# A fused sort-attention and feed-forward kernel: the first two chunks' calls in a new order

## The chip, the cores and the metric

The kernel runs on one core of one Trainium2 chip. The metric is the device time of one execution in microseconds (us), as the median of several runs. Before the change it is 232.17 us (three runs, 232.09 to 232.53). One further execution was recorded by the hardware profiler; every duration below comes from that one.

The core has five engines that run side by side, each with its own list of instructions that it works off in order: PE (matrix products, into the accumulator memory PSUM), DVE (elementwise work and reductions), ACT (activation functions and copies), POOL (memory fills, gathers of columns, and the start of most loads) and SP (which only starts DMAs). They wait for each other by semaphores. DMAs run on 16 DMA engines; those that POOL starts stand in one queue, those that SP starts in another.

## The reference

```python
P = sort_net                                  # 4 batches x 8 heads x 8 x 8
for _ in range(5):                            # balancing
    P = exp(P - max(P, -1)); P /= sum(P, -1); P /= sum(P, -2)
k_sorted = einsum('bhij,bhjcd->bhicd', P, k)  # 8 blocks of 96 keys, mixed by P
v_sorted = einsum('bhij,bhjcd->bhicd', P, v)
scores = q_block @ k_sorted_block.T / 8       # within each block of 96
attn = softmax(scores)
x = (attn @ v_sorted), heads side by side     # 3072 x 512
h = x @ w_in                                  # 512 x 2048
out = (h * cos(h)) @ w_out                    # 2048 x 512
```

## The kernel before, in words

The 3072 output rows are made in eight chunks of 384 rows (`n` = 0 to 7; two chunks to a batch). A chunk has four units `u` of 96 rows, which are one block of the attention over all eight heads.

For each unit: scores on PE (`s_ps`), their maximum and the subtraction on DVE (`s_max`, `s_sub`), the exponential on ACT (`expo`), a transposition on PE (`p_ps`) that ACT or DVE copies out of PSUM (`p_ev`), the product with the values on PE (`av_products`), the division on DVE (`av_norm`), and a second transposition (`x_ps`, `x_ev`), which leaves the unit's 96 columns in `xT`. For each chunk then the first feed-forward product `h` on PE, its cosine on ACT, the product of both on DVE (`gg`), and the second product `o`, whose result ACT or DVE copies and SP stores. In chunk 0 the first product is cut into halves of 192 columns: `up_four(h, g, part)`, with `h` = 0 for units 0 and 1 and `h` = 1 for units 2 and 3; `cos_four` and `gate_four` follow, and `down_four` is a quarter of the second product.

Keys and values are sorted by PE too. `kp` makes the first batch's sorted keys (48 products), which `k_place` copies from PSUM, `v0` the first batch's values (copied out by `v0e`), `ks` the second batch's keys (`kse`), and `v_sort_b` the second batch's values. Values of the upper half of the columns are first gathered into rows by POOL (`v_permute`).

The order of the work up to the second feed-forward stage is a list of calls, written out by hand: each call puts its instructions at the end of the lists of the engines it uses. PSUM tiles come from two pools, `big` (three buffers, `*B`) and `acc` (two buffers, `*C`); a call that takes a buffer waits until its last user is done. Behind that list, loops over chunks (`moe_up`, `moe_down`) with fixed slots give the order; they are not touched.

What the list of calls also sets is the order in which POOL starts loads: keys `kbuf` and values `vbuf` (both are parts of `kv`), the queries of chunk 1, 2 and 3 (`load_q`, the last in eight pieces), `w_in` and `w_out` in quarters, and the keys and values of batches 2 and 3 (`pair`, and thirds of `kv`). The built program gives eight semaphores in turn to the DMAs that POOL starts, so a DMA start carries a wait for the landing of the DMA that stood eight places before it. POOL also clears what must be zero: `z_turned(z)` clears the unused halves of `q_turned[z]`, the turned queries of every second chunk, which the full-height scores read (lines 142 to 145), `p_pads` the pads of the probability buffers (743), `z_vperm` the half of `vperm` (739), `zeros_between` the gaps between the queries of chunk 3 (137). `q_turned[0]` holds chunk 0's queries and, from `q_transpose(2, ...)` on, chunk 2's; its first full-height reader is `qk_half(2, 0, 0)`, behind `up(1, 2)` in the untouched part.

`keep_warm(times, ...)` issues products of a tile of zeros with itself; a `fill` argument of a call does so in that call's PSUM tile before its own products.

Of the kernel before, what the change touches and what calls it, by code (L numbers as in the profile page):

```python
# [10 lines left out]
FP32 = mybir.dt.float32  # L11
# [7 lines left out]
def kernel(  # L19
# [15 lines left out]
    nc = tc.nc  # L35
# [12 lines left out]
    IC = 4  # L48
# [698 lines left out]
    def kp(t, pool, tag, fill=0):  # L747
        o = ps["k", t] = pool.tile([128, 16, 2 * NB], FP32, name="ks", tag=tag)
        keep_warm(fill, o[:, :8].rearrange("p t n -> p (t n)"))
        for z in range(16):  # L750
            k_products(o, z, t * 16 + z, slice(0, 128),
                       bds[0][:, H:].rearrange("p x i -> p (x i)"))

    def k_place(t, eng, half=None):
        lo, hi = (0, nb) if half is None else (half * IC, half * IC + IC)
        o = ps["k", t]
        copy_on(
            eng, kT[0].rearrange("p z (h i) t -> p z h i t", i=nb)[
                :, ::2, :, lo:hi, t * 16:t * 16 + 16],
# [147 lines left out]
    v_permute(slice(0, 64), 48, False, 8, 56)  # L907
    v_permute(slice(0, 64), 56, False, 8, 64)
    k_place(2, A, 1)
    k_place(2, V, 0)  # L910
    kp(1, *B)
    k_place(0, A, 0)
    blocks.append(block([pick[:, :, z * PB:(z + 1) * PB] for z in (1, 0)]))
    k_place(1, V, 0)
    k_place(1, A, 1)
    values_matrix()
    k_place(0, A, 1)
    s_ps(0, 0, fill=3)
    v0(4, *C)
    s_max(0, 0)  # L920
    v0(0, *B)
    v0e(4, A)
    s_sub(0, 0)
    s_ps(0, 3)
    v0e(0, A)
    v0(5, *C)
    s_max(0, 3)
    load_w_out(0)
    v0e(5, A)
    s_ps(0, 1)  # L930
    load_w_out(1)
    load_w_out(2)
    load_w_out(3)
    v0(6, *C)
    ones(0)
    expo(0, 0, True)
    s_ps(0, 2)
    s_sub(0, 3)
    v0(1, *C)
    v0e(6, A)  # L940
    s_max(0, 1)
    expo(0, 3, True)
    v0(3, *B, fill=2)
    s_sub(0, 1)
    v0e(1, A)
    p_ps(0, 0, *C, fill=2)
    v0e(3, A)
    s_max(0, 2)
    v0(7, *C)
    expo(0, 1, True)  # L950
    kxp(2)
    v0(2, *B, fill=1)
    p_ev(0, 0, V)
    v0e(7, A)
    s_sub(0, 2)
# [299 lines left out]
```

## Time and profile before

| | before |
|---|---|
| median of three runs | 232.17 us (232.09 to 232.53) |
| the profiled execution's own time | 231.61 us |
| its span, first to last instruction | 229.8 us |
| PE busy | 220.8 us, 96% of the span |
| DVE, ACT, POOL busy | 170.8, 154.4, 96.1 us |
| start of the untouched part, `up(1, 0)` | 56.3 us |

The page of the profile gives busy time by engine, the chain of work that ended last, and the costliest groups of instructions. In a timeline, each row has the start, the duration, the engine, the source line and the operation with its tiles (out<-in), and in brackets the idle time of that engine before it with what ended it. A row with "x8" merges eight neighbours of a kind. "DMA to landing" is the time from the start on the issuing engine to the last byte.

### The profile page before, as it was taken

The numbers are of one execution on the slowest core, as the hardware profiler recorded it, in microseconds if no ns is written. First come the engines' busy times: TensorE is split into PE (matmuls) and PEld (weight loads), VectorE is DVE, ScalarE is ACT, GpSimd is POOL, SyncE is SP. The second block draws the span as 40 slices with busy tenths as digits, with TensorE's granted clock in tenths as the row PEclk, the third lists the DMA queues.
The fourth block names the chain that finished last, engine by engine and source line by source line (L and its number), as shares of the span: only waits on it lengthen the run. The fifth ranks groups of instructions, "written<-read, shape, count | busy, mean of one in ns | idle before, by whom it ended". The sixth has DMA issues, their size and how long they took to land.

```text
span 229.8 us, 5513 instructions
## 1 busy us (share of the span) xinstructions
PE 220.8 (96%) x2245; PEld 138.7 (60%) x2268; DVE 170.8 (74%) x291; ACT 154.4 (67%) x207; POOL 96.1 (42%) x121
## 2 busy tenths in 40 slices
PE   8788999999999999999999999999999999999994
PEld 3378898567765566655665456655655565556554
DVE  6769968978698778868489977987699769646700
ACT  5659877777889858797688466736674667716521
POOL 7999999399950197943609000800000000000000
PEclk9999999999999999999999999999999999999999
DMA  6999999994999799667979939964924440351012
GB/s 83 225 187 207 202 206 236 195 227 148 124 124 191 171 139 148 118 135 146 162 118 163 135 74 148 210 98 81 206 92 80 90 160 0 69 147 46 0 46 94
DMA packets 67833, 31.21 MB, mean 136 GB/s; under 512 B 56416, under 2 KB 63200, under 8 KB 67552
## 3 DMA queue, kind: packets, MB, share of 16 engines
q0 software_dynamic: 24048, 13.64, 43.3%
q1 hardware_dynamic: 43472, 17.02, 35.1%
q8 instruction: 18, 0.29, 0.5%
q10 hardware_dynamic: 288, 0.20, 0.3%
q14 instruction: 7, 0.06, 0.1%
HBM read 27.27 MB, written 6.29 MB: 146 GB/s over the span
## 4 chain that ended last, share of the span: by engine, by line
PE 90%; DVE 3%; POOL 2%; issue 1%; ACT 1%; POOLq 0%; ACTq 0%
PE h L672 32%; PE o L697 30%; PE h L860 5%; PE o L881 4%; PE av L628 4%; PE sc L441 3%; PE ks L408 2%; PE o L1219 2%; PE pps L838 1%; PE sc L507 1%; PE xps L659 1%; PE vs L785 1%; PE vs L452 1%; PE qps L268 1%; PE xps L847 1%
## 5 line engine op out<-in xcount | busy, mean ns | idle before, releaser
L672 PE MATMUL h<-xT,w_in_t 128*128 128x384 bf16 x448 | 78.4, 326 | 0.1
L697 PE MATMUL o<-w_out_t,gg 128*128 128x512 bf16 x303 | 73.7, 379 | 1.0 <-issue 0.3
L676 ACT ACTIVATE c<-h,half_pi 128x768 f32<-128x768 f32 x56 | 50.5, 902 | 26.0 <-PE h L672 25.0
L680 DVE TENSOR_TENSOR gg<-c,h 128x768 bf16<-128x768 f32 x56 | 52.7, 949 | 19.5 <-ACT c L676 19.5
L672 PEld LDWEIGHTS <-w_in_t 128*128 128x128 bf16 x448 | 42.2, 98 | 26.3 <-DVE xT L259 0.6
L697 PEld LDWEIGHTS <-gg 128*128 128x128 bf16 x320 | 29.0, 99 | 28.3
L573 ACT ACTIVATE p_buf<-s 96x768 bf16<-96x768 f32 x32 | 26.6, 843 | 5.2 <-DVE s L494 4.0
L179 POOL COPY vperm<-kv 64x768 bf16<-64x768 bf16 (+2 forms) x12 | 28.4, 2416 | 3.9 <-DMA kv<-in_v_dram 3.9
L494 DVE TENSOR_TENSOR s<-sc,mx 96x384 f32<-96x384 f32 (+1 forms) x33 | 24.3, 735 | 1.6
L492 DVE TENSOR_REDUCE mx<-sc 96x4 f32<-96x384 f32 (+1 forms) x33 | 24.0, 729 | 0.2 <-PE sc L507 0.2
L641 DVE TENSOR_TENSOR xn<-av,r 96x512 bf16<-96x512 f32 x32 | 22.0, 687 | 1.1
L129 POOL DMA_DIRECT2D kv<-in_q_dram x24 | 16.0, 676 | 0.7 <-issue 0.7
L257 ACT COPY kv<-o 128x512 f32<-128x512 f32 (+2 forms) x10 | 5.2, 524 | 14.1 <-PE o L697 11.5
L257 ACT CAST kTs<-ks 128x512 bf16<-128x512 f32 (+1 forms) x18 | 11.0, 630 | 5.3 <-PE ks L408 4.4
L639 DVE RECIPROCAL r<-av 96x8 f32<-96x8 f32 x32 | 6.4, 199 | 9.6 <-PE av L628 9.1
L129 POOL DMA_DIRECT2D q_mem<-in_q_dram x16 | 10.7, 687 | 2.0 <-DMA kv<-in_v_dram 1.5
L881 PE MATMUL o<-w_out_t,gg 128*128 128x512 bf16 x45 | 11.2, 379 | 0.2
L259 DVE COPY kv<-o 128x512 f32<-128x512 f32 (+1 forms) x5 | 3.1, 612 | 11.1 <-PE o L1219 8.5
L860 PE MATMUL h<-xT,w_in_t 128*128 128x192 bf16 x128 | 11.1, 246 | 0.0
L441 PE MATMUL sc<-kTs,q_turned 128*128 128x96 bf16 x152 | 11.1, 206 | 0.0
L599 POOL CAST held<-q_turned 96x1 f32<-96x1 bf16 x2 | 0.4, 184 | 24.3 <-DMA q_turned<-q_mem 16.3
L860 PEld LDWEIGHTS <-w_in_t 128*128 128x128 bf16 x128 | 10.5, 98 | 0.0
(134 smaller groups left out, 285.6 us busy)
## 6 DMA issues: line engine op xcount, KB each, us to landing
out_dram<-kv SPq DMA_DIRECT2D x12, 256.0 KB, 2.7
out_dram<-o_s SPq DMA_DIRECT2D x10, 256.0 KB, 3.5
w_in_t<-in_moe_w_in_dram POOLq DMA_DIRECT2D x4, 512.0 KB, 11.7
w_out_t<-in_moe_w_out_dram POOLq DMA_DIRECT2D x4, 512.0 KB, 12.3
kv<-in_k_dram POOLq DMA_DIRECT2D x2, 768.0 KB, 9.8
kv<-in_v_dram POOLq DMA_DIRECT2D x2, 768.0 KB, 12.9
pair<-in_k_dram POOLq DMA_DIRECT2D x2, 768.0 KB, 12.3
kv<-in_v_dram POOLq DMA_DIRECT2D x6, 256.0 KB, 5.3
```

The costliest lines, as they stand in the source:

```text
L129: nc.gpsimd.dma_start(out=q_heads[:, i, :, e], in_=src[:, ih * IC + i, :, e])
L179: nc.gpsimd.tensor_copy(dst, src)
L492: nc.vector.reduce_max(mx[:], scv, axis=AX.X)
L494: nc.vector.tensor_tensor(s, scv, mx.to_broadcast(list(s.shape)), op=ALU.subtract)
L573: nc.scalar.activation(p[:, :, :blk], s_t.pop((n, u)).rearrange("p e h c -> p (e h) c"), AF.Exp, scale=scale)
L641: nc.vector.tensor_tensor(xn.rearrange("p h e d -> p e h d"), avv[:, :, :, :D], r.to_broadcast([blk, 2, H2, D]), op=ALU.mult)
L672: nc.tensor.matmul(h[:, f2, :w], w_in_t[:, kk, f * 128:(f + 1) * 128], xT[n][:, kk], start=(kk == 0), stop=(kk == KC - 1))
L676: nc.scalar.activation(c[:], h[:, :, :w], AF.Sin, bias=half_pi[:, 0:1])
L680: nc.vector.tensor_tensor(gt[n, fp // 2][:, f:f + 2], c[:], h[:, :, :w], op=ALU.mult)
L697: nc.tensor.matmul(o[:], gt[n, f // 4][:, f % 4, ts * 128:(ts + 1) * 128], w_out_t[:, f, :], start=(f == 0), stop=(f == FC - 1))
L860: nc.tensor.matmul(o[:, part, f2 * w:(f2 + 1) * w], w_in_t[:, kk, f * 128:(f + 1) * 128], xT[0][:, kk, h * w:(h + 1) * w], start=(kk == 0) ...
L881: nc.tensor.matmul(out_ps[ts][:], gt[0, q][:, f % 4, ts * 128:(ts + 1) * 128], w_out_t[:, f, :], start=(f == 0), stop=(f == FC - 1))
```

## The change

Three things change; arithmetic and sizes of all products of data stay as they are.

**The list of calls for chunks 0 and 1 has a new order.** Chunk 0's units 0 and 1 go through scores, values and transposition before units 2 and 3, the `h` = 0 half of the first product starts behind units 0 and 1, the second batch's keys (`ks`) are sorted between chunk 0's first products instead of behind chunk 1's attention, and chunk 1's units run in the order 2, 3, 1, 0 (before: 1, 0, 3, 2). The loads and clears on POOL stand where their calls now stand. The matrix for the values (`block`, `spread`) is made before the sorted keys, and the ones beside the values are set by DVE instead of POOL (`vS`).

**The first sorted keys take four PSUM tiles** of 16, 8, 8 and 16 products, 48 in all, in place of three of 16.

**No products of zeros behind the balancing**: the `fill` arguments are gone, and with them ten products. Those during the balancing stay.

```diff
-    blocks = [block([pick[:]])]
+    blocks = [block([pick[:]]), block([pick[:, :, z * PB:(z + 1) * PB] for z in (1, 0)])]
     spread(bds[0], blocks[0], xs=slice(H, 2 * H))
-
-    def values_matrix():
-        spread(bdv, blocks[1], xs=slice(0, H))
-        spread(bds[0], blocks[0], xs=slice(0, H))
-        spread(bdv, blocks[1], xs=slice(H, 2 * H))
+    spread(bdv, blocks[1], xs=slice(0, H))
+    spread(bds[0], blocks[0], xs=slice(0, H))
+    spread(bdv, blocks[1], xs=slice(H, 2 * H))
+    nc.vector.memset(vS[0][:, :, D:D + 1], 1.0)
...
-    def kp(t, pool, tag, fill=0):
-        o = ps["k", t] = pool.tile([128, 16, 2 * NB], FP32, name="ks", tag=tag)
+    def kp(c, n, pool, tag, fill=0):
+        o = ps["k", c] = pool.tile([128, n, 2 * NB], FP32, name="ks", tag=tag)
...
-    kp(2, *B)
-    kp(0, *B)
+    kp(16, 8, *B)
+    k_place(16, A, 0)
+    kp(32, 16, *B)
+    kp(24, 8, *C)
...
-    s_ps(0, 0, fill=3)
...
-    z_turned(0)
-    cos_four(0, 0)
-    p_pads()
...
+    p_pads()
+    av_norm(1, 0, True)
+    z_turned(0)
```

**Where it moves instructions, first place: POOL between the load of the second batch's keys and the pieces of chunk 3's queries.** Before, the clears of `q_turned[0]` (here `q_turned_94`) and of the pads stood ahead of the `pair` loads:

```order
L739 MEMSET vperm 64x3072
L142 MEMSET q_turned_94 64x1568
L143 MEMSET q_turned_94 64x1568
L144 MEMSET q_turned_94 64x32
L145 MEMSET q_turned_94 64x32
L743 MEMSET p_buf_107 96x8x32
L743 MEMSET p_buf_108 96x8x32
L743 MEMSET p_buf_109 96x8x32
L119 DMA q_mem<-in_q_dram 96x8x256
L92 DMA pair<-in_k_dram 128x3072 x2
L179 COPY vperm<-kv 64x1536 x4
L137 MEMSET kv 96x16x64 x2
```

Now, on the same engine, with what each row waits for (DMASW0 to DMASW7 are the eight semaphores of POOL's DMAs; the rows before these are the loads of `pair`, of chunk 2's queries and `v_permute`):

```order
L92 DMA kv<-in_v_dram 128x1024 [waits DMASW3_49]
L129 DMA kv<-in_q_dram 96x4x64 [waits DMASW4_49,PE_49]
L129 DMA kv<-in_q_dram 96x4x64 [waits DMASW5_49,PE_49]
L129 DMA kv<-in_q_dram 96x4x64 [waits DMASW6_49]
L129 DMA kv<-in_q_dram 96x4x64 [waits DMASW7_49,PE_49]
L129 DMA kv<-in_q_dram 96x4x64 [waits DMASW0_49]
L129 DMA kv<-in_q_dram 96x4x64 [waits DMASW1_49]
L129 DMA kv<-in_q_dram 96x4x64 [waits DMASW2_49]
L129 DMA kv<-in_q_dram 96x4x64 [waits DMASW3_49]
L428 CAST held<-kTs 128x1 [waits DMAHW2_49,DMAHW1_49]
```

```order
L742 MEMSET p_buf_107 96x8x32
L742 MEMSET p_buf_108 96x8x32
L742 MEMSET p_buf_109 96x8x32
L142 MEMSET q_turned_94 64x1568 [waits Pool_49]
L143 MEMSET q_turned_94 64x1568
L144 MEMSET q_turned_94 64x32
```

The second piece follows the first without a row between. The clear of `q_turned[0]` went from ahead of the `pair` loads to behind the eight pieces of chunk 3's queries; the last four pieces wait for the second `pair` half (DMASW0) and for the three thirds of `kv` (DMASW1 to DMASW3), which are loads that stand eight places ahead of them. Before, those thirds stood behind the eight pieces.

**Second place: PE, at the first products of `qk_half(2, 0, 0)`,** the full-height scores of chunk 2 in the untouched part. Before:

```order
L452 MATMUL vs_1363<-bdv_153,vperm_88 96x64
L441 LDWEIGHTS q_turned0_94 [waits DMAHW5_49,DMAHW4_49]
L441 MATMUL sc_1374<-kTs_98,q_turned0_94 128x96 [waits Activation_49]
L441 LDWEIGHTS q_turned0_94
L441 MATMUL sc_1374<-kTs_98,q_turned0_94 128x96
```

and now:

```order
L451 MATMUL vs_1356<-bdv_153,vperm_88 96x64
L440 LDWEIGHTS q_turned0_94 [waits DMAHW2_49,DMAHW1_49,Pool_49]
L440 MATMUL sc_1367<-kTs_98,q_turned0_94 128x96 [waits Activation_49]
L440 LDWEIGHTS q_turned0_94
L440 MATMUL sc_1367<-kTs_98,q_turned0_94 128x96
```

The row has a wait for POOL that it did not have; in the built program it is the wait for the first clear of `q_turned[0]` (line 142), which PE had long passed before.

**Third place: DVE, from the first scores to unit 1's copy into `xT`.** Before:

```order
L824 TENSOR_REDUCE mx<-sc 96x8
L259 COPY pT<-pps 96x768
L828 TENSOR_TENSOR s<-sc,mx 96x8x2x48
L259 COPY pT<-pps 96x768
L639 RECIPROCAL r<-av 96x8
L641 TENSOR_TENSOR xn<-av,r 96x2x4x64
L639 RECIPROCAL r<-av 96x8
L641 TENSOR_TENSOR xn<-av,r 96x2x4x64
L639 RECIPROCAL r<-av 96x8
L641 TENSOR_TENSOR xn<-av,r 96x2x4x64
L639 RECIPROCAL r<-av 96x8
L641 TENSOR_TENSOR xn<-av,r 96x2x4x64
```

and now:

```order
L823 TENSOR_REDUCE mx<-sc 96x8
L827 TENSOR_TENSOR s<-sc,mx 96x8x2x48 x2
L638 RECIPROCAL r<-av 96x8
L640 TENSOR_TENSOR xn<-av,r 96x2x4x64
L638 RECIPROCAL r<-av 96x8
L640 TENSOR_TENSOR xn<-av,r 96x2x4x64
L259 COPY pT<-pps 96x768
L259 COPY xT<-xps 128x4x96
```

The copies of units 0's and 1's probabilities left DVE (ACT has them now), and the divisions of units 0 and 1 with unit 1's copy into `xT` stand right behind the last score step, ahead of units 2's and 3's divisions.

More of the change, by code (lines that the diff above doesn't have):

```diff
@@ L979 @@
[L979 to L989 removed]
+    p_ev(0, 0, A)
+    p_ps(0, 1, *C)
+    av_products(0, 0)
+    s_sub(0, 2)
+    av_norm(0, 0, True)
+    load(kbuf, 0, kin_d[1])
+    picks(pick_pair, (2, 3))
+    last = block([pick_pair[:]], *C)
+    p_ev(0, 1, A)
+    av_products(0, 1)
@@ L990 @@
+    av_norm(0, 1, True)
+    x_ps(0, 0, *C)
+    expo(0, 3, True)
+    p_ps(0, 3, *B)
+    load(vbuf, 64, vin_d[1])
+    p_ev(0, 3, V)
+    x_ps(0, 1, *B)
+    x_ev(0, 1, V)
+    expo(0, 2, True)
+    p_ps(0, 2, *B)
+    spread(bds[1], last)
+    p_ev(0, 2, V)
+    av_products(0, 3)
+    x_ev(0, 0, A)
+    up_four(0, 0, 0)
+    up_four(0, 0, 1)
+    kxp(0)
+    av_products(0, 2)
+    av_norm(0, 3, True)
+    x_ps(0, 3, *C)
     up_four(0, 3, 0)
     up_four(0, 3, 1)
-    z_turned(0)
+    av_norm(0, 2, True)
```

324 lines of the change are left out of this document (147 added, 177 removed).

## The prediction

> **What bounds the kernel now.** I read the summary of busy shares first, then the chain that ended last, then the table by stretches, then the DMA queues. In the table a row has the length of the stretch, the busy time of PE, PEld, DVE, ACT and POOL (with counts), the granted clock, the DMA share and GB/s.
>
> ```profile
> span 229.8 us, 5513 instructions
> PE 220.8 (96%) x2245; PEld 138.7 (60%) x2268; DVE 170.8 (74%) x291; ACT 154.4 (67%) x207; POOL 96.1 (42%) x121
> PE 90%; DVE 3%; POOL 2%; issue 1%; ACT 1%; POOLq 0%; ACTq 0%
> 15.00:20.00 5.00, 4.41 (x104) 3.56 (x104) 4.68 (x9) 4.28 (x8) 5.00 (x5) 1.00 1.24 207
> 20.00:25.00 5.00, 4.74 (x78) 4.39 (x78) 4.78 (x8) 4.63 (x8) 4.82 (x9) 1.00 1.31 203
> 55.00:60.00 5.00, 5.00 (x94) 3.72 (x91) 4.36 (x8) 4.60 (x8) 4.94 (x7) 1.00 0.71 149
> ```
>
> PE is busy for 96% of the span and is 90% of the chain. Only the front has gaps: between 15 and 25 us PE is idle for 0.59 + 0.26 = 0.85 us while DVE is busy for 9.46 of 10, so DVE helps to set the pace there. Later, as at 55 to 60, PE has none. An instruction that reaches PE earlier in the front is therefore worth its time at the end, and a wait of PE later costs its full length. A second resource is full in the same stretch, the software DMA queue that POOL feeds (over the first 70 us):
>
> ```profile
> q0 software_dynamic: 10810, 11.27, 98.3%
> ```
>
> What is loaded there comes in order of issue at the queue's speed, whatever PE does.
>
> **The change, first term: the front.** It removes the products of zeros and takes copies off DVE's line to the first expert product. Rows of the groups by form (12 to 27 us), of PE's timeline at the start, of the chain in order of time, and of DVE's timeline:
>
> ```profile
> L246 PEld LDWEIGHTS <-warm 128*128 128x128 bf16 x10 | 0.8, 104 | 0.1
> L246 PE MATMUL vs<-warm 128*128 128x512 bf16 x2 | 0.8, 378 | 0.0
> 7.28 0.82 PE L246 MATMUL idle<-warm 128*128 128x512 bf16 x3
> 26.06 0.26 PE av L628 x8
> 26.98 0.50 PE qps L268 x16
> 27.48 0.28 PE xps L847 x4
> 27.75 3.30 PE h L860 x40
> 37.66 0.30 PE bl L386 x8
> 22.39 0.54 DVE L259 COPY pT<-pps 96x768 bf16<-96x768 bf16 x1
> 22.86 0.94 DVE L828 TENSOR_TENSOR s<-sc,mx 96x768 f32<-96x768 f32 x1
> 24.51 0.20 DVE L639 RECIPROCAL r<-av 96x8 f32<-96x8 f32 x1
> 25.35 0.19 DVE L639 RECIPROCAL r<-av 96x8 f32<-96x8 f32 x1
> 28.03 0.34 DVE L259 COPY xT<-xps 128x384 bf16<-128x384 bf16 x1
> ```
>
> The first row counts the ten by their weight loads. Three 512-column products take 0.82 us and one alone 0.38, so one more costs 0.22; six of them and four of half the columns (0.11) are 1.76 us of PE. What of it reaches the path is read from DVE. Its eight score steps end at 22.86 + 0.94 = 23.80 now; with one copy of 0.54 out from between them and some 0.25 of a sooner first step they end at 23.0. Two divisions at the pitch 25.35 - 24.51 = 0.84 follow (24.7), then the copies of 0.54 and 0.34 that the first `up_four` needs: it starts at 25.6 and not at 27.75, 2.1 sooner. But not all of this is saved. In the new order the products for unit 3's average, an x transpose and the query products come behind that point: 0.26 + 0.28 + 0.50, less the block of 0.30 that moves ahead, is 0.74 owed. I subtract 0.26 more for the short waits that a new interleaving usually leaves (an estimate, about a third of the 0.85 idle above), and PE is **1.1 us earlier** from then on. Bounds: 0.6 where the waits equal the present 0.85 again, and 1.76 where all zeros were on the path.
>
> **Second term: POOL's clear of `q_turned[0]`, which decides.** The first score product of `qk_half(2, 0, 0)` gets a wait for POOL's clear at line 142. PE, POOL and the queue as they are now (timelines):
>
> ```profile
> 61.22 0.33 PE L441 MATMUL sc<-kTs,q_turned 128*128 128x96 bf16 x4
> 62.94 0.34 PE L441 MATMUL sc<-kTs,q_turned 128*128 128x96 bf16 x4
> 35.07 1.40 POOL L142 MEMSET q_turned<- 64x1568 bf16 x1
> 38.19 0.82 POOL L743 MEMSET p_buf<- 96x256 bf16 x3
> 39.80 1.10 POOL L92 DMA_DIRECT2D pair<-in_k_dram  x2
> 44.40 11.29 POOL L179 COPY vperm<-kv 64x1536 bf16<-64x1536 bf16 x4 [3.50 <-DMA kv<-in_v_dram]
> 62.93 0.19 POOL L429 CAST held<-kTs 128x1 f32<-128x1 bf16 x1
> 87.59 0.67 POOL L129 DMA_DIRECT2D q_mem<-in_q_dram  x1 [1.53 <-DMA kv<-in_v_dram]
> ```
>
> Before, the clear is over at 36.5, 25 us ahead of its reader. Now it stands behind `v_permute` (11.29), the second `pair` half, `z_vperm`, three thirds of `kv` and eight pieces of queries. The last row shows what that means: a piece is issued on one of eight semaphores used in turn, and waited 1.53 us for the load of `kv` eight issues ahead. Here the last piece waits in the same way for the last third to land; call that moment T. Behind it come the piece (0.67), the cast (0.19), three pads (0.82 together) and the clear (1.40), with 0.24 from landing to issue (worked out below): T + 3.3.
>
> T goes by the queue. Landings, from the views of one line each (shortest, median and longest of the loads issued in a window): line 119 (issued at 12.8), 164 (19.7 to 22.0), 88 (29.0 and 29.6), 92 at 39.8 and 40.3, and 92 at 79.7 to 80.7; issue rows from POOL's timeline:
>
> ```profile
> 12.76 0.82 POOL L119 DMA_DIRECT2D q_mem<-in_q_dram  x1
> DMA to landing us min/median/max: 14.1/14.1/14.1
> 19.74 2.98 POOL L164 DMA_DIRECT2D w_out_t<-in_moe_w_out_dram  x4
> DMA to landing us min/median/max: 9.7/12.3/15.3
> 29.57 0.55 POOL L88 DMA_DIRECT2D kv<-in_v_dram  x1
> DMA to landing us min/median/max: 11.7/13.2/14.7
> DMA to landing us min/median/max: 10.4/12.3/14.2
> 79.68 1.59 POOL L92 DMA_DIRECT2D kv<-in_v_dram  x3 [0.27 <-issue]
> DMA to landing us min/median/max: 4.0/4.9/6.6
> kTs<-kTs SPq DMA_DIRECT2D x2, 192.0 KB, 2.9
> ```
>
> The query load landed at 12.76 + 14.1 = 26.9; the second `pair` half (issued at 40.3, the longest of its two) at 40.3 + 14.2 = 54.5. In these 27.6 us the queue carried four `w_out` quarters, keys and values of chunk 1, queries 2 and two `pair` halves, 5.5 MB or 199 KB/us. The new order carries these and then the three thirds. `v_permute` can start when chunk 1's values land; they are issued ahead of `w_out` now, so 2 MB sooner. It ends near 45 (44.3 less 2 MB at 199 KB/us, 34, and 11.29), and the thirds are issued behind it and `z_vperm` near 49, before the queue has emptied at 54.5 - 3.9 (a 768 KB half at 199 KB/us) = 50.6. So it does not run dry and T is the sum of bytes. Three thirds of 256 KB: chunk 1's keys and values, 1536 KB, landed from 37.3 (22.0 + 15.3) to 44.3 (29.6 + 14.7), 219 KB/us and 1.17 a third, 3.5 in all. At the worst rate, that of the thirds around 80 us, whose first landed at 79.7 + 4.0 = 83.7 and whose last, issued at 80.7, at 87.35, two more took 1.8 each: 5.4. (The issue of the waiting piece at 87.59 gives the 0.24.) The two `k_swap` copies of 192 KB, on SP's queue, which are now started behind this stretch, move into it: 0 if the engines take them in the gaps, their bytes at 219 KB/us, 1.75, if not; I take 0.9, the half, since the queue is full but transfers of SP shared it before. A third store on that queue that now falls in: 0.3 (0 to 0.6). T = 54.5 + 3.5 + 0.9 + 0.3 = **59.2**; by the ends, 26.9 + 5504/219 + 3.5 = 55.5 and 54.5 + 5.4 + 1.75 + 0.6 = 62.3.
>
> The clear is done at 59.2 + 3.3 = 62.5. PE arrives at 61.2 - 1.1 = 60.1, waits 2.4 us, and goes on 1.3 us later than before. The first term is swallowed: POOL's time does not hang on PE's. Everything of PE stands behind this row in its one order, the expert products of the earlier chunk too, and with them ACT and DVE, which live on them; PE has no gap later to win it back. The second half's clear (1.40 later) is done before its reader, 62.94 - 61.22 = 1.72 later. Sum: 231.61 (this profiled execution; its span is 229.8) + 1.3 = 232.9. The median of the runs shown is 0.56 over that execution, so **233.5**.
>
> Two edits cost nothing: the copies moved to ACT (busy 4.28 and 4.63 of 5 in the front) could make ACT late by at most the 0.54, and a late quarter of `w_out` could hold the first down products; both delay PE ahead of 60 us, under 2.4 us of cover. Without that cover each would cost up to 0.5.
>
> [...]
>
> **The rivals.**
> B, the queue drains in time: T is under 57, near the 55.5 by the rate of keys and values, PE finds the clear done or nearly so, and the first term stands: 232.17 - 1.1 = 231.1, faster. For it speaks that the present stretch includes packets of other queues and slower small rows; against it, that the same packets come again. It decides from T = 57.9 downwards (61.2 - 3.3).
> C, the two terms cancel: T between 57.4 and 58.4, within 0.46 us (0.2%, about what a measurement of this kernel tells from no change), 232.2.
> D, the queue at its worst: T of 61 or more, clear at 64.3 to 65.6, +3.1 to +4.4, up to 236.6.
> E, the clock of PE falls without the zeros:
>
> ```profile
> 1.00 5.16 PE L246 MATMUL idle<-warm 128*128 128x512 bf16 x14 [1.00 <-DVE warm L231]
> 9.33 0.53 PE L323 MATMUL qps<-ident,q_mem 96*64 96x96 bf16 x16 [1.23 <-ACT q_turned L329]
> ```
>
> The first fourteen products take 0.37 each, later ones 0.22: a cold stretch of that length costs 14 x 0.15 = 2.1 us. In the front it would make PE arrive at 62.2, still before 62.5; it would turn B into 233.2. Against it: PE was idle for 1.23 us at 8 to 9 us and the granted clock stays 1.00 in every stretch above, and the new gaps, 0.85 + 1.76 spread over ten us, are each shorter. After the wait at 60 it would come on top of A, and that is D's price too.
> [...]
> F, the change does not do what it says, and the first `up_four` starts no sooner: PE arrives at 61.2, still before 62.5, and the time is again 233.5.
>
> **How the numbers follow.** Likeliest, A (PE waits for the clear, net +0.5 to +3; F and E's front in it): 0.58. B: 0.20. C: 0.14. D: 0.08. Time 233.5; A's own range 232.7 to 235.2. The range reaches down to B's 231.1, and up to T = 61.1, the forecast and 1.9: 231.0 to 235.4. Faster 0.20, within 0.2% 0.14, slower 0.58 + 0.08 = 0.66.
>
> **What would show it.** First `up_four` at 25 to 26.2 confirms the first term's start; PE up to 0.6 to 1.8 sooner at the last product ahead of `qk_half(2, 0, 0)`. That product's idle column naming POOL's clear (line 142) with 1 to 5 us is the second term; POOL's last query piece with an idle that names the DMA of `kv` near 59 is its cause. If that piece is issued before 57, my queue sum is wrong and B holds. If the first piece already waits, or POOL is late from `v_permute`, the chain is right with another cause. If PE's wait is there and the end does not move, PE's later gaps, which I call none, were read wrongly.

## The result, and the profile after

The changed kernel takes **235.38 us** (median of 6 runs, 234.79 to 236.35), the kernel before 232.16 (6 runs beside it): ratio 1.0141, 95% interval 1.0117 to 1.0165, **3.2 us slower**. The forecast was 233.5, 1.3 slower. The profiled execution took 234.79.

The page of the changed kernel, its first lines and its chain of waits:

```profile
span 233.0 us, 5498 instructions
PE 222.2 (95%) x2237; PEld 140.3 (60%) x2258; DVE 172.7 (74%) x295; ACT 152.3 (65%) x206; POOL 95.2 (41%) x120
PEclk9997799999999999999999999999999999999999
PE 64%; POOL 14%; DMA 12%; issue 4%; ACT 3%; POOLq 0%; ACTq 0%
```

PE has eight products fewer than before (ten zeros went, some records are missing from each trace) and yet more busy time, 222.2 against 220.8 us. The third line says why: the granted clock, full in all of before, is down to 0.7 in two of the forty slices. The chain, 90% PE before, is now only 64% PE, with 26% on POOL and DMA. These lines point at two different causes, and the rest of this document is about which one counts.

The table by stretches of 1 us (columns as in the prediction: length, busy time of PE, PEld, DVE, ACT, POOL, granted clock, DMA, GB/s):

```profile
16.00:17.00 1.00, 1.00 (x16) 0.96 (x16) 0.97 (x2) 1.00 (x3) 1.00 (x1) 1.00 1.25 215
17.00:18.00 1.00, 0.50 (x10) 0.32 (x8) 1.00 (x2) 0.81 (x3) 1.00 (x2) 1.00 1.25 204
18.00:19.00 1.00, 0.19 (x14) 0.19 (x15) 0.62 (x1) 1.00 (x2) 1.00 (x2) 1.00 1.22 201
19.00:20.00 1.00, 1.00 (x25) 0.96 (x18) 0.75 (x1) 0.17 (x1) 1.00 (x1) 0.80 1.25 209
22.00:23.00 1.00, 1.00 (x16) 1.00 (x15) 1.00 (x2) 1.00 (x3) 0.93 (x2) 0.50 1.27 218
23.00:24.00 1.00, 0.67 (x11) 0.46 (x9) 1.00 (x2) 1.00 (x3) 1.00 (x2) 0.99 1.33 188
26.00:27.00 1.00, 0.87 (x14) 0.75 (x12) 0.93 (x3) 0.98 (x3) 1.00 (x3) 0.71 1.11 226
28.00:29.00 1.00, 1.00 (x8) 0.95 (x7) 0.92 (x3) 0.00 (x0) 0.96 (x3) 0.50 1.17 246
29.00:30.00 1.00, 1.00 (x9) 0.95 (x8) 0.00 (x0) 0.00 (x0) 1.00 (x2) 0.58 0.99 209
```

Between 17 and 19 us PE is busy for 0.69 of 2 us; the clock then falls to half at 19.6, is back at 23.0, falls again at 26.4 and is back at 29.8. In the second spell the `up_four` products run, of which 8 or 9 fit in a microsecond, where before had 15 or 16.

Where the time comes in is read from PE's timeline: the rows of the changed kernel up to the first score product of `qk_half(2, 0, 0)` and the first late wait, then rows of before for the same work.

```profile
59.31 0.41 PE L451 MATMUL vs<-bdv,vperm 128*128 128x64 bf16 x8
60.11 0.42 PE L451 MATMUL vs<-bdv,vperm 128*128 128x64 bf16 x8 [0.38 <-DVE q_turned L259]
60.37 1.47 PE L671 MATMUL h<-xT,w_in_t 128*128 128x384 bf16 x8
63.22 0.41 PE L451 MATMUL vs<-bdv,vperm 128*128 128x64 bf16 x8
63.80 0.34 PE L440 MATMUL sc<-kTs,q_turned 128*128 128x96 bf16 x4 [0.17 <-POOL q_turned L142]
107.76 0.43 PE L627 MATMUL av<-vS,pT 96*128 96x65 bf16 x8 [0.22 <-DMA pT<-p_buf]
```

```profile
57.62 0.66 PE L452 MATMUL vs<-bdv,vperm 128*128 128x64 bf16 x16
58.12 1.46 PE L672 MATMUL h<-xT,w_in_t 128*128 128x384 bf16 x8
```

At the first `v_sort_b` product PE is 59.31 - 57.62 = 1.69 us late; behind the second, which waits for DVE to empty a buffer, 60.37 - 58.12 = 2.25; at the score product 63.80 - 61.22 = 2.58; at the end, after a wait for a transposed `pT` and a last fraction, 233.0 - 229.8 = 3.2.

POOL, in its own timeline of the changed kernel, does what was forecast:

```profile
55.46 0.67 POOL L129 DMA_DIRECT2D kv<-in_q_dram  x1 [1.92 <-DMA pair<-in_k_dram]
57.14 0.67 POOL L129 DMA_DIRECT2D kv<-in_q_dram  x1 [1.01 <-DMA kv<-in_v_dram]
59.10 0.67 POOL L129 DMA_DIRECT2D kv<-in_q_dram  x1 [1.29 <-DMA kv<-in_v_dram]
60.64 0.67 POOL L129 DMA_DIRECT2D kv<-in_q_dram  x1 [0.88 <-DMA kv<-in_v_dram]
62.34 1.40 POOL L142 MEMSET q_turned<- 64x1568 bf16 x1
```

The last four pieces wait for the loads eight issues ahead, and the clear ends at 63.74. But PE's idle time there is 0.17 us, not 2.4: its product before that ended at 63.22 + 0.41 = 63.63, so PE had come at 63.63 by itself.

### The profile page after: what moved, and what is told of

The parts are those of the page before. It is cut to its first block, busy times and chain, and to the rows that moved or that the text cites. A ratio compares the mean times of both kernels' runs of the same rounds, so it can differ in the third digit from the quotient of the medians.

```text
span 233.0 us, 5498 instructions
## 1 busy us (share of the span) xinstructions
PE 222.2 (95%) x2237; PEld 140.3 (60%) x2258; DVE 172.7 (74%) x295; ACT 152.3 (65%) x206; POOL 95.2 (41%) x120
## 4 chain that ended last, share of the span: by engine, by line
PE 64%; POOL 14%; DMA 12%; issue 4%; ACT 3%; POOLq 0%; ACTq 0%
PE h L671 30%; PE o L696 24%; DMA kv<-in_v_dram 9%; POOL vperm L179 6%; DMA pT<-p_buf 4%; PE av L627 3%; PE sc L440 2%; PE o L1218 2%; POOL w_out_t L164 1%; POOL q_turned L142 1%; PE vs L784 1%; PE xps L658 1%; ACT L572 1%; ACT c L675 1%; POOL q_mem L119 1%
## 5 line engine op out<-in xcount | busy, mean ns | idle before, releaser
L675 ACT ACTIVATE c<-h,half_pi 128x768 f32<-128x768 f32 x56 | 50.4, 900 | 26.9 <-PE h L671 26.1
L671 PEld LDWEIGHTS <-w_in_t 128*128 128x128 bf16 x448 | 42.2, 98 | 26.3 <-DVE xT L259 0.6
L257 ACT CAST kTs<-ks 128x512 bf16<-128x512 f32 (+2 forms) x19 | 11.0, 594 | 3.9 <-PE ks L407 3.9
L859 PE MATMUL h<-xT,w_in_t 128*128 128x192 bf16 x128 | 12.7, 258 | 0.0
L859 PEld LDWEIGHTS <-w_in_t 128*128 128x128 bf16 x128 | 11.2, 104 | 0.2
L865 ACT ACTIVATE c<-h,half_pi 128x768 f32<-128x768 f32 x8 | 7.2, 901 | 5.8 <-PE h L859 5.8
```

Source lines behind the costliest of these rows:

```text
L257: eng.copy(dst, src)
L671: nc.tensor.matmul(h[:, f2, :w], w_in_t[:, kk, f * 128:(f + 1) * 128], xT[n][:, kk], start=(kk == 0), stop=(kk == KC - 1))
L675: nc.scalar.activation(c[:], h[:, :, :w], AF.Sin, bias=half_pi[:, 0:1])
L859: nc.tensor.matmul(o[:, part, f2 * w:(f2 + 1) * w], w_in_t[:, kk, f * 128:(f + 1) * 128], xT[0][:, kk, h * w:(h + 1) * w], start=(kk == 0) ...
```

## The experiments

**Two theories.** *Clear*: POOL's late clear sets where PE goes on, as predicted. *Clock*: PE's lost clock does, and the clear only happens to end at the same moment. The chain of waits in the changed kernel runs through the clear; it names the one that came last, by 0.11 us.

In the table, "late" is the start of the first `v_sort_b` product less 57.62, "idle" PE's idle time from 12 us to there and "clock" an upper bound of what the clock cost there (busy time times one minus the granted clock, summed over stretches of 1 us), "clear" PE's wait for line 142 at chunk 2's first score product, and "end" how late the last of the 448 products `h` of the untouched part starts (215.89 us in before), all from the profiled execution. What "end" has over "late" came in after that first `v_sort_b` product. Time is the median in us, the ratio is to before on the same chip.

| kernel | time | ratio, 95% | late | idle | clock | clear | end |
|---|---|---|---|---|---|---|---|
| before | 231.9 to 232.2 | | 0 | 1.61 | 0 | 0 | 0 |
| the change | 235.38 | 1.0141 (1.0117 to 1.0165) | 1.69 | 2.69 | 3.38 | 0.17 | 2.98 |
| e1 clear early | 235.17 | 1.0142 (1.0126 to 1.0158) | 1.39 | 2.20 | 3.31 | 0 | 3.01 |
| e2 zeros back | 234.88 | 1.0127 (1.0113 to 1.0141) | 2.55 | 1.37 | 3.33 | 0 | 3.11 |
| e3 both | 233.98 | 1.0085 (1.0071 to 1.0098) | 1.97 | 1.99 | 1.69 | 0 | 2.52 |
| e4 before, no zeros | 233.21 | 1.0054 (1.0033 to 1.0075) | 0.06 | 2.58 | 0 | 0 | 1.16 |
| e5 clear early, 25 zeros | 234.26 | 1.0097 (1.0082 to 1.0111) | 0.82 | 0.96 | 0 | 0 | 2.72 |
| e6 25 zeros | 234.67 | 1.0120 (1.0101 to 1.0138) | 1.04 | 1.25 | 0 | 0.51 | 3.04 |
| e7 before, clear late | 240.75 | 1.0372 (1.0346 to 1.0398) | 0.19 | 1.24 | 0 | 6.77 | 9.13 |
| e8 as e5, buffers swapped | 233.48 | 1.0067 (1.0053 to 1.0080) | 1.22 | 1.34 | 0 | 0 | 2.19 |
| e9 clear early, swapped, zeros 22 to 27 us | 231.66 | 0.9988 (0.9979 to 0.9997) | 0.04 | 1.92 | 0 | 0 | 0.03 |
| e10 clear early, swapped | 234.70 | 1.0122 (1.0106 to 1.0137) | 1.42 | 2.38 | 3.30 | 0 | 3.18 |
| e12 20 small products | 234.34 | 1.0104 (1.0090 to 1.0118) | 0.88 | 2.33 | 1.71 | 0.41 | 2.64 |
| e13 as e9, clear late | 235.18 | 1.0122 (1.0095 to 1.0148) | 0.05 | 2.08 | 0 | 2.80 | 4.29 |
| e14 as e9, values later | 238.33 | 1.0272 (1.0251 to 1.0294) | 4.91 | 6.12 | 1.65 | 0 | 7.41 |
| e15 as e9, zeros 22 to 24 us | 232.23 | 1.0011 (0.9998 to 1.0024) | 0.11 | 2.73 | 0 | 0 | 0.56 |
| e16 as e9, zeros 25 to 27 us | 232.52 | 1.0017 (0.9998 to 1.0035) | 1.05 | 2.16 | 1.70 | 0 | 1.37 |

### First round: each suspect taken away

**e1**, the clear early:

```diff
     load_pair(pair, kin_d, 0 * CD // 2, 1 * CD // 2)
+    z_turned(0)
...
     av_norm(1, 0, True)
-    z_turned(0)
```

> The changed kernel with one call moved: the clear of q_turned[0] (z_turned(0)) stands right behind the second pair half instead of behind chunk 3's query pieces, 13 us earlier. In the changed kernel two things meet at 63.8 us: PE's clock was down to half twice between 19.8 and 30 us, so that PE was 1.76 us late at 50 us, and POOL's clear of q_turned[0] ended at 63.74, where PE takes up its score product at 63.80, 2.58 us later than before. Clock theory (the lost clock carries the result, the wait hides nothing but 0.2 us): the time stays at 235.0 to 235.4. Clear theory (the wait carries it): 231 to 232. Both, each sufficient: 234.5 to 235.4, the wait for POOL gone.

The wait for POOL is gone and the time is 235.17, the change's own to 0.2 us. The clear alone, once the clock is lost, is worth next to nothing: the clear theory in its plain form falls. In the profile PE is 0.65 us ahead of the change behind the score product (1.94 us late against 2.59) and loses that again further on, the largest part, 0.42, in a wait for a transposed `pT` at 80.8 us.

**e2**, the zeros back at the calls that had them, and **e3**, both edits:

```diff
-    s_ps(0, 0)
+    s_ps(0, 0, fill=3)
... likewise v0(3) 2, p_ps(0, 0) 2, v0(2) 1, av_products(0, 3) 2
```

> The changed kernel with the ten products of zeros back at the same calls (three at the first scores, two at v0(3), two at p_ps(0, 0), one at v0(2), two at av_products(0, 3)); the late clear stays. Clock theory: the granted clock stays at or near 1.00 between 15 and 30 us, PE is about 1 us ahead of before at 50 us, and the time is 231 to 232.5. Clear theory, and both-sufficient: PE is ahead at 50 us but waits 2 to 3.5 us for POOL's clear near 61 to 64 us, and the time is 234.5 to 235.4. If the clock falls all the same, the zeros are not what held it.

> Both edits: the clear early and the zeros back. Clock theory, clear theory and both-sufficient all give 231 to 232.3 (the front's gain of about 1 us less up to 0.8 for zeros on the path). If it stays above 234, a third cause is at work; together with the two runs beside it, it is the corner that tells a sum (each edit gives its part) from a maximum (only both together give anything).

Both expectations assumed that the ten zeros would hold the clock. They don't, in the new order: in e2 it falls at 24.6 us for 6.8 us, in e3 at 26.8 for 3.4. So e2 tells nothing of the clear. e3, with one spell less, is 1.2 us faster than e1, but this is no measure of the clock: at the first `v_sort_b` product e3 is the later one (1.97 against 1.39 us), and e1 falls behind it only by 1.07 us that come in from 79 us on, where e3 loses nothing. The clock stayed in play, but the zeros had to go elsewhere.

**e4**, the kernel before without its zeros:

```diff
-    s_ps(0, 0, fill=3)
+    s_ps(0, 0)
... likewise v0(3), p_ps(0, 0), v0(2), av_products(0, 3)
```

> The kernel before with the ten products of zeros left out and nothing else changed. If the zeros hold the clock in any order, the granted clock falls below 1.00 between 15 and 30 us and the time is 2 to 3 us over before (234 to 235). If the old order has few enough gaps, the clock stays and the time is 230.5 to 232.2. Where PE's idle time at 18 us that no releaser explains (0.26 in before, 1.00 in the changed kernel, both times in front of about the 443rd of PE's instructions) comes from the loading of code at a time of its own, that idle grows here to 0.5 to 1.2 and ends again between 18.4 and 18.9 us.

The clock stays at 1.00, and PE is 0.06 us late at the first `v_sort_b` product: from 12 us to there PE's busy time fell from 44.01 to 43.10 us and its idle time rose by 2.58 - 1.61 = 0.97. The zeros had stood in gaps. That the kernel is 1.3 us slower all the same comes later, where a transposed `pT` is late (rows of e4):

```profile
104.12 1.03 PE L697 MATMUL o<-w_out_t,gg 128*128 128x512 bf16 x4
105.72 0.43 PE L628 MATMUL av<-vS,pT 96*128 96x65 bf16 x8 [0.57 <-DMA pT<-p_buf]
```

The kernel before has no such wait; the `pT` transfers issued there between 98 and 106 us took 2.8 us (median) to land. Why the one in e4 is late, with a front that is 0.06 us off, was not found: it shows that a kernel can lose a microsecond behind the front ("end" 1.16) with a full clock and no late clear. PE's stop at 18 us did not grow as expected: no idle time without a releaser shows there at all.

### Second round: the clock held by force

**e5** has the early clear, the zeros back and fifteen more where PE stood idle, 25 in all (the expectation below says eleven; the edit has fifteen, and the trace 25 weight loads for them); **e6** the same zeros with the late clear; **e8** is e5 with the two `q_transpose` buffers of chunk 2 in the old order.

```diff
-    v0(2, *C)
+    v0(2, *C, fill=3)
-    p_ps(0, 1, *C)
+    p_ps(0, 1, *C, fill=4)
-    av_products(0, 0)
+    av_products(0, 0, fill=2)
-    x_ps(0, 0, *C)
+    x_ps(0, 0, *C, fill=3)
-    x_ps(0, 1, *B)
+    x_ps(0, 1, *B, fill=2)
-    p_ps(0, 2, *B)
+    p_ps(0, 2, *B, fill=2)
```

and in e8 beside it

```diff
-    q_transpose(2, 0, (V, V), *B)
-    q_transpose(2, 1, (V, V), *C)
+    q_transpose(2, 0, (V, V), *C)
+    q_transpose(2, 1, (V, V), *B)
```

> The changed kernel with the clear early, the zeros back and eleven more of them where PE still stood idle between 17 and 27 us (before v0(2), p_ps(0, 1), av_products(0, 0), both x transposes of units 0 and 1, p_ps(0, 2)). With the early clear and the ten zeros the clock still fell once, from 26.9 to 30.1 us, in front of the first up_four, and PE stood 1.97 us late at the first v_sort_b product. Clock theory: here it stays at 1.00 through 30 us, that lateness falls to 0.2 to 0.8 us, and the time is 232.2 to 233. If the clock stays and the lateness is still over 1.5, the clock was not what cost. If the clock falls, idle time alone does not set it.

> The same zeros, with the clear late as in the change: the changed kernel at a full clock. Clear theory: PE reaches the first score product of chunk 2 near 62 us and waits 1.5 to 2.5 us for POOL's clear, which ends near 63.7; the time is 234.3 to 235. Clock theory alone: no such wait, 232.2 to 233 as in the run beside it. The difference of these two runs is the price of the late clear at a full clock.

> The early clear and all the zeros, and the two q_transpose calls of chunk 2 take their accumulator buffers in the old order (acc, then big, where the change has big, then acc). In the changed kernel the second v_sort_b product waits 0.38 us for DVE's copy out of the buffer of q_transpose(2, 1), and PE's lateness grows there from 1.69 to 2.25 us, which every run with the new order shows and none with the old. Expected: that wait is gone, and the time is 0.3 to 0.6 under the run with the early clear and all the zeros. If the wait only moves to another row, no difference.

The clock is at 1.00 in all three and e5's lateness falls from e3's 1.97 to 0.82, as the clock theory says. The time does not follow (234.26, above e3's 233.98): the `q_turned` wait of 0.38 us is still there, and e5 loses 1.35 us more at 161 and 208 us, most of it in a wait for `xT` of 0.90, where e3 loses nothing. That 25 zeros take room of their own is likely (e9 below has 13 and is 0.04 late), but not measured apart. e8 takes the `q_turned` wait away and is 0.78 us faster. e6 against e5 gives the clear 0.4 us, with a wait of 0.51: PE was 1.6 us late already, so most of the clear was covered.

**e7** puts only the late clear into the kernel before: three thirds, the pieces, `p_pads` and `z_turned(0)` in the change's order.

```diff
-    z_turned(0)
     cos_four(0, 0)
-    p_pads()
...
+    load_pair(vbuf, ...) three thirds
+    load_q(3)
+    hold_keys()
+    p_pads()
+    z_turned(0)
     q_transpose(2, 0, (V, V), *C)
     q_transpose(2, 1, (V, V), *B)
     zeros_between(3)
-    load_q(3)
-    hold_keys()
-    load_pair(vbuf, ...) three thirds
```

> The kernel before with one thing of the change: the clears of q_turned[0] and of the pads stand behind chunk 3's query pieces, and these behind the thirds of the values; the zeros and the order of the front stay. The clock should stay at 1.00. Clear theory: POOL's last piece waits for the last third, which lands at 60 to 61.5 us; the clear ends 3.3 us later, PE idles 2 to 3.5 us at its first score product of chunk 2 (61.2 in before), and the time is 234 to 235.5. If PE does not wait there, or the time stays under 232.7, the step on the late clear in the prediction is wrong in itself.

PE's row of e7 at the place, and two stretches of 5 us:

```profile
68.34 0.50 PE L441 MATMUL sc<-kTs,q_turned 128*128 128x96 bf16 x4 [6.77 <-POOL q_turned L142]
65.00:70.00 5.00, 1.66 (x9) 0.99 (x10) 1.09 (x2) 0.00 (x0) 4.58 (x9) 0.59 0.75 50
70.00:75.00 5.00, 5.00 (x40) 3.16 (x39) 2.22 (x5) 2.54 (x4) 3.62 (x4) 0.73 0.53 98
```

The mechanism is there by itself, and larger than expected, for in before `v_permute` ends at 55.7 and the thirds are issued only then. The clear ends at 68.3, the clock falls in the wait, and the time is 8.8 us up.

### Third round: fewer zeros, in the right place

**e9**: early clear, swapped buffers, and of the zeros only thirteen; **e10**: the same without zeros. Against e8:

```diff
-    s_ps(0, 0, fill=3)
+    s_ps(0, 0)
... likewise none at v0(2), v0(3), p_ps(0, 0), av_products(0, 3);
... left in e9: p_ps(0, 1) 4, av_products(0, 0) 2, x_ps(0, 0) 3, x_ps(0, 1) 2, p_ps(0, 2) 2
```

> The early clear, the buffers of q_transpose swapped back, and only the zeros from p_ps(0, 1) to p_ps(0, 2) (22 to 27 us); none earlier, so that PE's gap at 18 us stays. Clock theory in its finer form: of the two stretches at half clock (19.8 to 23.2 and 26.7 to 30 us) the first costs little, because PE waits there for other engines, and the second costs about 1.6 us, because the dense products of up_four run in it. Here the first stays, the second goes, and PE's lateness at the first v_sort_b product is 0 to 0.7 us (1.39 without any zeros, 0.82 with all); time 232.2 to 233.2, under every version of the change so far. If the lateness is over 1.2, the first stretch costs as well.

> The early clear and the buffers of q_transpose swapped back, no zeros. Against the early clear alone (235.17): the step of 0.55 us at the second v_sort_b product is gone; 234.4 to 234.8. The clock falls twice as there, and PE is 1.2 to 1.8 us late at 57.6 us. The difference to the run with the late zeros beside it is what the clock costs after 26 us.

Thirteen zeros make 234.70 - 231.66 = **3.0 us** of difference, and the clock is at 1.00 in e9 where e10 has both spells (mean clock 0.998 or more in ten of e9's eleven runs, 0.985 or less in all five of e10's). But only 1.42 - 0.04 = 1.4 us of it stands at the end of the front, where the clock was lost. Another 1.76 ("end" less "late") come in later in e10, at 79, 107 and 183 us, the largest at this wait, and not at all in e9:

```profile
79.29 0.43 PE L627 MATMUL av<-vS,pT 96*128 96x65 bf16 x8 [0.91 <-DMA pT<-p_buf]
```

Whether these belong to the lost clock is not shown; e4 has 1.1 us of such losses at a full clock. e9 is faster than the change by 3.7 us and than before by 0.26 (ratio 0.9988): the fastest kernel here, by little. The finer part of the expectation was wrong: the first spell went too, though the zeros stand behind it. PE's rows of e9 and of e10 at that place, in that order, have the same instructions ahead of them and different stops:

```profile
17.99 0.40 PE L803 MATMUL sc<-kTs,q_turned 64*128 64x64 bf16 x16 [0.26 <-issue]
```

```profile
18.57 0.40 PE L803 MATMUL sc<-kTs,q_turned 64*128 64x64 bf16 x16 [1.12 <-issue]
```

**e11** moves the two `k_swap` copies (with `hold_keys`) behind the query pieces.

```diff
-    k_swap(kT[1])
...
-    hold_keys()
...
+    k_swap(kT[1])
+    hold_keys()
     q_transpose(2, 0, (V, V), *B)
```

> The changed kernel with the two 192 KB copies of chunk 1's keys (k_swap) on SP behind the query pieces, as late as in before. POOL's last query piece went at 60.64 us in the changed kernel, because the last third of the values landed at 60.4. If the copies take their full bytes from the same DMA engines (384 KB at 219 KB/us, 1.75 us), that piece goes at 58.6 to 59.2; if half (0.9, the prediction's value), at 59.5 to 60; if they fit into gaps, at 60.4 or later. The time of the kernel should not fall by more than 0.3, since PE itself arrives near 63.6.

The last query piece, and above it the start of `v_permute` in the change and in e11, ahead of the place where the copies stood:

```profile
34.74 11.35 POOL L179 COPY vperm<-kv 64x1536 bf16<-64x1536 bf16 x4 [0.29 <-DMA kv<-in_v_dram]
34.37 11.33 POOL L179 COPY vperm<-kv 64x1536 bf16<-64x1536 bf16 x4 [0.69 <-DMA kv<-in_v_dram]
59.26 0.67 POOL L129 DMA_DIRECT2D kv<-in_q_dram  x1 [1.07 <-DMA kv<-in_v_dram]
```

The last piece goes 60.64 - 59.26 = 1.38 us sooner. But `v_permute`, which starts when chunk 1's values land, is already 34.74 - 34.37 = 0.37 us sooner, and so is every load up to the last quarter of `w_out`: e11's loads were issued earlier, with PE's front. The copies account for the rest, **1.0 us**, about the half that the prediction took (0.9) and not the full bytes (1.75). The expectation, which compared the whole 1.38, did not allow for this. It is one execution; it took 234.31, 1.1 under the change and so more than the 0.3 that was expected, but its clock fell only once and PE was 0.47 us late at the first `v_sort_b` product, so the time says nothing of the copies.

**e12** adds 20 products of one column at 11 us.

```diff
             q_twice(3)
             idle(2)
+            keep_warm(20, big.tile([128, 512], FP32, name="idle", tag="big"), 1)
```

> The changed kernel with 20 products of one column (40 instructions of PE) in the balancing, at 11 us, where PE waits anyway. In every run so far PE stands still without a releaser after 444 matmuls and weight loads together, whichever call that is, and goes on between 18.1 and 18.8 us. If this is the loading of PE's code at a time of its own, the stop comes again after about 444, so 40 instructions earlier in the program (in v0(2) or v0(7), not at the scores of unit 3), lasts 1.0 to 2.0 us and ends again between 18 and 19. If it belongs to the scores of unit 3 itself, it stays there, at about 484. The time moves by less than 0.7 us either way.

PE's row of e12:

```profile
16.88 0.31 PE L785 MATMUL vs<-bdv,vperm 128*128 128x64 bf16 x4 [0.69 <-issue]
```

The stop has moved into `v0(4)`, 4 + 8 + 8 = 20 products ahead of unit 3's scores, where the change has it: earlier by as many as were put in. In this run it followed the count. It does not end at a time of its own, as I had expected: it ended at 16.88. With a shorter stop the clock fell only once, and the time moved by 1.0 us, more than expected.

### Fourth round: what was still open

**e13**: e9 with the clear late, as in the change:

```diff
-    z_turned(0)
...
     av_norm(1, 0, True)
+    z_turned(0)
```

> The kernel of e9 (buffers swapped back, zeros from 22 to 27 us, clock at 1.00, PE 0.04 us from its time before at chunk 2's first score product) with the clear of q_turned[0] late again as in the change. This is the prediction's main case without the loss of clock. Clear theory: PE comes at 61.3, POOL's clear ends at 63.2 to 63.8, PE waits 1.9 to 2.6 us; the time is 1.9 to 2.8 us over e9: 233.6 to 234.5. If it stays under 232.4, the late clear is harmless and the prediction's second term is wrong.

```profile
64.23 0.50 PE L440 MATMUL sc<-kTs,q_turned 128*128 128x96 bf16 x4 [2.80 <-POOL q_turned L142]
64.00:65.00 1.00, 0.77 (x6) 0.60 (x7) 0.23 (x1) 0.00 (x0) 0.94 (x2) 0.50 0.00 0
67.00:68.00 1.00, 1.00 (x16) 0.75 (x15) 0.00 (x0) 0.68 (x1) 1.00 (x2) 0.93 0.00 0
```

This is the prediction's main case, PE on time (0.05 late) and a full clock: it waits 2.80 us, and here the clock falls at the end of the wait, for 3.4 us in all. In two of the four runs a spell was lost (235.54 and 235.99, mean clock 0.993), in two none (234.47 and 234.81, 1.000). Against e9 the clear costs **3.1 us** by the two ratios (1.0122 and 0.9988 of 232), 3.5 by the medians.

**e14** loads chunk 1's values behind `w_out`:

```diff
-    load(vbuf, 64, vin_d[1])
...
     load_w_out(3)
+    load(vbuf, 64, vin_d[1])
```

> The kernel of e9 with the load of chunk 1's values behind the four quarters of w_out instead of ahead of them. In e9 PE waits 0.34 us at 46.2 us for a quarter of w_out. Expected: that wait is gone (the quarters land 3.5 us sooner) and the time falls by 0.2 to 0.4, to 231.2 to 231.5; v_permute starts up to 3.5 us later, which nothing on PE should notice now that the clear is early. If PE then waits for chunk 3's queries or for v_sort_b, the time rises instead.

```profile
62.53 1.09 PE L451 MATMUL vs<-bdv,vperm 128*128 128x64 bf16 x16 [4.36 <-POOL vperm L738]
```

Wrong: `v_permute` waited 10.65 us for its values, `z_vperm` behind it (and behind the clear) became late, and PE waited 4.36 for that. POOL's chain from these values on has little slack for any reader, not only for the clear.

**e15** and **e16** keep part of e9's zeros, six at 22 to 24 us or seven at 25 to 27:

```diff
e15:
-    x_ps(0, 0, *C, fill=3)
+    x_ps(0, 0, *C)
... likewise x_ps(0, 1), p_ps(0, 2)
e16:
-    p_ps(0, 1, *C, fill=4)
+    p_ps(0, 1, *C)
... likewise av_products(0, 0)
```

> The kernel of e9 with only the zeros at p_ps(0, 1) and av_products(0, 0), 22 to 24 us (six of 256 columns). If the clock is set by how busy PE is in the 3.4 us in front of each step, these six suffice to hold it in the second stretch or not: with the clock at 1.00 the time is 231.4 to 231.9; with one fall at 26 to 27 us it is 233 to 234. The fall at 19.8 us lies ahead of these zeros and cannot depend on them, unless the stop after 444 instructions changes its length.

> The kernel of e9 with only the zeros at the two x transposes and at p_ps(0, 2), 25 to 27 us (five of 192 and two of 256 columns). Same alternatives: 231.4 to 231.9 if they hold the clock, 233 to 234 with one fall, 234.4 or more with two.

The six earlier ones hold the clock in most runs (0.998 to 1.000 in eight of ten) and the kernel is level with before, at 232.23 a little over the time expected. The seven later ones, right ahead of the dense products, do not: the clock is at 1.000 in one run of ten, and the profile shows one fall, at 24.8 us. The time was expected at 233 to 234 with one fall and is 232.52. Sorted by the mean clock, the runs of this one kernel give the price of a spell without any change of instructions: 231.75 with a full clock (one run), 231.62 to 232.98 with 0.990 or 0.993, about one spell (seven runs, 232.49 in the middle), 233.70 with 0.983, about two (one run; the tenth, 235.24 at 0.985, is not in the ratio). So one spell cost some 0.7 us and two some 2, each from few runs.

**What the runs settle.** Without zeros and with the clear late 235.38 (the change), without zeros and with the clear early 235.17 (e1; 234.70 in e10), zeros in place and the clear late 235.18 (e13), both mended 231.66 (e9; e9, e10 and e13 have the swapped buffers, whose own part is 0.47, e1 to e10). The late clear alone costs 3.1 to 3.5 us, the missing zeros alone 3.0, and together they cost it once, since one covers the other. The zeros' part goes through the clock for 1.4 us; how the rest comes about, in waits for transposed tiles behind the front, stays open.

## Why the prediction was right or wrong

**The direction and the second term's mechanism were right.** POOL's last piece waited for the last third, and T + 3.3 held to 0.1 us: T was 60.64 - 0.24 = 60.4, the clear's end 63.74. The term that was mis-sized is T, 60.4 where I had 59.2: the pieces that wait for thirds went 1.96 and 1.54 us apart, so a third took 1.75 us and not 1.17. The bound of 1.8 that I had set as the worst was the real one. The three thirds took 5.2 us (the second `pair` half landed at 55.46 - 0.24 = 55.2) where the sum had 3.5 and 0.3 for a store; two stores of 256 KB landed in that time, at 58.3 and 60.2, but that they are the reason was not tested. The other terms held: 54.5 + 0.9 for the half behind the `k_swap` copies gives 55.4, and the copies cost 1.0 (e11).

The 1.2 us of T are most of what the forecast lacks. With the clear at 63.74, the prediction's own sum gives 63.74 - 61.22 = 2.5 us, and PE is 2.58 late there in the trace, 3.2 at the end, against a forecast of 1.3. That the sum comes out so well with T put right is in part luck: PE came at 63.63 by itself, and would have been nearly as late with the clear at the forecast 62.5.

**The first term failed at its step "its eight score steps end at 23.0".** In the changed kernel they end at 22.85 + 1.81 = 24.66 (DVE's rows; the last one is e9's):

```profile
19.25 0.95 DVE L823 TENSOR_REDUCE mx<-sc 96x8 f32<-96x768 f32 x1 [0.64 <-PE sc L803]
21.97 0.95 DVE L823 TENSOR_REDUCE mx<-sc 96x8 f32<-96x768 f32 x1 [0.90 <-PE sc L803]
22.85 1.81 DVE L827 TENSOR_TENSOR s<-sc,mx 96x768 f32<-96x768 f32 x2
21.59 1.81 DVE L827 TENSOR_TENSOR s<-sc,mx 96x768 f32<-96x768 f32 x2
```

I had summed DVE's durations as if it never waited. In the new order two units' scores stand behind three and more `v0` products each, so DVE waits 1.54 us for PE, and in the first of these waits PE itself stands still for 1.00. With a full clock and a stop of 0.26 (e9) the steps end at 23.40; the other 1.26 us go with the longer stop and the half clock. Nor did the zeros' 1.76 us count: e4 shows that they lay in gaps. Even at a full clock, with the first `up_four` a microsecond sooner (26.64 in e9, 27.59 in before) and not the 2.1 forecast, PE is at 0.04 by the first `v_sort_b` product: the missing 1.1 us is the whole of the first term.

**Rival E was waved off on the wrong evidence.** I gave it as a 2.1 us price that the wait would cover, and argued from a single idle stretch of 1.23 us without a fall. It happened twice over, PE came not at 60.1 but at 63.63, and so the wait that was forecast at 2.4 is 0.17 in the trace. Of these 3.5 us, 1.1 is the first term that did not come, 1.4 goes with the zeros and the clock (e10 against e9), 0.55 with the buffers of `q_transpose`; some 0.5 is not assigned. F, that the first `up_four` starts no sooner, came true with it (27.80). That neither would change the time while the clear is late was nearly right: the price of the clock went under the cover of the clear, and e1 shows the same from the other side.

**"PE has no gap later" was a little wrong.** From 2.58 us late at the score product PE goes to 3.2 at the end, about 0.4 of it at the wait for a transposed `pT` at 107.76 us; e1, e4 and e10 lose 1.1 to 1.8 us at such places. The new wait of 0.38 us at the second `v_sort_b` product, from the two `q_transpose` buffers that changed places, was not in my list.

What would have been the right sum for the case as forecast is e13: 3.1 to 3.5 us over e9, of which 2.8 is the wait and the rest, in half its runs, the clock behind it. D priced that addition (a long wait, and then the clock) but set it at the far end of T, and 0.08.

## What to carry to other kernels

A chain of waits names the last of several causes: here the clear came 0.11 us behind PE's own lateness, and taking it away gained nothing until the second cause was gone too, so remove suspects in pairs before you call one harmless. Products that compute nothing can still be load-bearing: before deleting them, compare the granted clock with and without them in stretches of 1 us, and where it falls put some back in PE's idle time (13 of them made 3.0 us here; six at 22 to 24 us mostly held the clock, seven at 25 to 27 mostly did not). Compare late starts at several points of the kernel, since what is gained in one place can be lost again in another that the edit never touched. When an instruction is moved behind DMA issues on its engine, look at which landings those wait for: here they waited for loads eight issues ahead, and a clear of 1.4 us ended 63.74 - 36.47 = 27 us later than before.

## What the runs showed of the hardware

**The clock fell without a long idle stretch.** From 12 us to the first fall the longest stop of PE was 1.00 us in the change and 1.12 in e10; in before a stop of 1.23 us, at 8.1 to 9.3 us, was followed by no fall, and in e13 the clock was at 0.50 at the end of a wait of 2.80. The two spells of the change last 3.41 us each, with 3.42 at a full clock between them:

```profile
16.19:19.60 3.41, 2.10 (x42) 1.84 (x39) 2.74 (x4) 2.79 (x5) 3.41 (x3) 1.00 1.24 207
19.60:23.01 3.41, 3.41 (x54) 3.26 (x53) 2.51 (x4) 2.67 (x5) 2.32 (x4) 0.50 1.25 209
23.01:26.43 3.42, 2.54 (x47) 2.00 (x46) 3.35 (x7) 3.42 (x6) 3.33 (x7) 1.00 1.46 236
26.43:29.84 3.41, 3.41 (x33) 3.30 (x34) 2.33 (x6) 1.37 (x2) 3.33 (x6) 0.50 1.00 210
```

In the tables by 1 us of the other runs the time at half clock between 16 and 31 us adds up to 3.4 us in e3, e11, e12, e14 and e16 and to 6.8 in e1 and e10, once or twice a spell of the change.

What made the clock fall was not shown. PE's busy time at the place does not tell the cases apart: from 17 to 19 us it is 0.69 of 2 us in the change and 0.85 in e10, and the clock falls; it is 0.74 in e15 (its two rows below, against 0.50 and 0.19 above), and the clock stays at 1.00. Nor was it shown why e13 and e16 lose a spell in one execution and none in another.

```profile
17.00:18.00 1.00, 0.43 (x9) 0.31 (x8) 1.00 (x2) 0.96 (x3) 1.00 (x2) 1.00 1.24 202
18.00:19.00 1.00, 0.31 (x16) 0.28 (x16) 0.57 (x1) 0.98 (x2) 1.00 (x2) 1.00 1.25 206
```

**PE stopped with no releaser between 16 and 19 us, in 14 of the 18 profiled executions** (not in e4, e5, e7 and e8), for 0.22 (e2) to 1.13 us (e1). In the change 221 matmuls and 223 weight loads are recorded ahead of the product that ends the stop. In each of the twelve executions with the change's order and no products put in ahead of 12 us it comes behind 136 recorded matmuls from 12 us on, whether products of zeros are among them (e2, e3, e6: the stop lies in `v0`) or not (the others: at unit 3's scores), and it came 20 products earlier when 20 were put in at 11 us (e12). What PE waited for was not shown, nor why the stop is 1.12 us in e10 and 0.26 in e9 behind the same instructions.
